# Decode attention: a slot's scores in four 32-column tiles, the maximum across quadrants by GpSimd, and no waits of TensorE on itself

## The chip, the cores and the metric

The kernel runs on one core of a Trainium2 chip. The metric is device time in microseconds; the time before is the median of three runs.

## The reference

Two layers of decode attention, each followed by a dense MLP, for a batch of 8 with one new token per row. Both layers use the same weights and the same K and V caches.

```python
def attention(x, k_cache, v_cache, wq, wo):      # x: 8 x 1 x 512
    q = (x @ wq).reshape(8, 1, 32, 128)          # 32 query heads of 128
    k = jnp.repeat(k_cache, 4, axis=1)           # 8 KV heads, 8192 keys each, 4 query heads per KV head
    v = jnp.repeat(v_cache, 4, axis=1)
    p = softmax(q . k * 128 ** -0.5)
    return (p . v) @ wo
x = x + attention(layernorm(x)); x = x + silu(layernorm(x) @ w1) @ w2     # w1: 512 x 1792
x = x + attention(layernorm(x)); x = x + silu(layernorm(x) @ w1) @ w2
```

All inputs are bfloat16. K and V hold 134 MB each. What must be computed for every one of 8 x 8 (batch row, KV head) pairs and both layers is a softmax over 8192 keys for 4 query heads.

## The kernel before

**Tasks, positions, slots.** A task is one (layer, batch row, KV head): 128 tasks in all, in an order that `make_tasks` writes out, with the two layers interleaved. A task's 8192 keys are four granules of 2048 keys (`NGRAN`), each granule fills a 512 KB slot of an arena in SBUF with 27 slots (`NSLOT`), and each slot has two halves of 1024 keys. The main loop (L722) goes over positions `p`, one half each, so a task has eight positions. Of the 32 granules of keys of a batch row, the last 18 (`KEEP`) stay in the arena from layer 0 to layer 1, already transposed; a layer-1 task on those heads loads V alone.

**Loads.** All loads of K and V are issued by SyncE (L326, called from `issue`), in an order that `plan_loads` fixes beforehand by the position at which each is needed. K is needed `LT` = 3 positions ahead of its scores, V is used `LP` = 14 positions after its scores. Each load waits until the former content of its slot has been used; `issue_until(p)` at the end of a position issues what may follow.

**What a position does,** in the order of emission:

- `emit_t_until(p + 3)`: eight 128x128 transposes of raw keys on TensorE into one of three PSUM banks (L420), then one copy of 128x1024 back over the slot's half, by VectorE (L428, five of eight) or ScalarE (L426, three of eight). Kept keys skip this.
- `emit_s(p)`: the scores of the half. Two matmuls (L455) with 512 keys as the moving operand each. The stationary operand is a window of 128 columns out of `QB`, in which a task's four query vectors stand 16 columns apart, with zeros between them; the window is shifted by the block's number j, so that block j's scores of query r land in PSUM row 16r + j, and the 16 matmuls of a task add up in one bank of 64 used rows by 512.
- `emit_pv(p - 14)`: eight matmuls (L517) of 128 stationary V columns against 32 moving columns of P.
- a softmax step of the task before, by phase: phase 0 the maximum (L464 to L474: a row maximum of 64x512 out of PSUM, then a 32x32 transpose, a small maximum, a scaling and a second transpose, all on VectorE, so that each row gets the maximum of its query); phase 1 the exp on ScalarE with the row sums (L478); phase 3 the sums (L484 on VectorE, then a sum across partitions on GpSimd, L487); phase 4 the transposes of P (L496) and their copy out of PSUM (L500); phase 7 the reciprocal (L504).
- where due, one step of a batch row's chain between the layers: output projection (L604), layer norm (L539 to L573, with two GpSimd reductions, L541 and L556), MLP and next queries (L586).

**Waits.** `Sync.acquire` (L90) collects, for every resource that an operation reads or writes, the marks of the last writer and of the readers since, keeps the highest mark per engine, and emits a wait for each, for the operation's own engine as well. Each engine takes its instructions in order.

Of the kernel before, what the change touches and what calls it, by code (L numbers as in the profile page):

```python
# [7 lines left out]
SM_SCALE = DH ** -0.5  # L8
# [19 lines left out]
PVN = 8  # L28
CW = 32
SETTLE = 2  # L30
ACT_EVAC = (1, 4, 7)

BF16 = mybir.dt.bfloat16
# [25 lines left out]
class Sync:  # L59
# [30 lines left out]
    def acquire(self, eng, reads=(), writes=()):  # L90
        toks = []
        for r in reads:
            if r.last_write is not None:
                toks.append(r.last_write)
        for r in writes:
            if r.last_write is not None:
                toks.append(r.last_write)
            toks.extend(r.reads)
        best = {}
        for t in toks:  # L100
            k = t.sem
            if k not in best or best[k].val < t.val:
                best[k] = t
        for t in best.values():
            self.wait(eng, t)

    def release(self, tok, reads=(), writes=()):
        for r in reads:
# [96 lines left out]
def _build(ctx, nc, A_x, A_k_cache, A_v_cache, A_wq, A_wo, B_w1, B_w2, out):  # L205
# [7 lines left out]
    NCH = S // 128  # L213
    NGRAN = NCH // (GRP * GPG)
    SLOT = GRP * GPG * 128
    assert GPT * GRP == NCH and NGRAN * GPG == GPT and KT * 128 == D and FT * 128 == F

    order = [(g, k) for g in range(HKV) for k in range(NGRAN)]
    kept = set(order[len(order) - KEEP:])
# [14 lines left out]
    def sb(shape, dt, name):  # L234
        _cnt[0] += 1
        return ctx.enter_context(nc.sbuf_tensor(f"{name}_{_cnt[0]}", shape, dt))
# [19 lines left out]
    w2_sb = sb([128, FT, D], BF16, "w2")  # L256
    ident = sb([128, 128], BF16, "ident")
    XT = [sb([128, KT, B], BF16, f"XT{n}") for n in range(3)]
    NJ = NCH * 128 // KB
    NR = NJ * REP  # L260
    CPB = KB // 128
    JPG = GRP * 128 // KB
    assert NR <= 128 and NJ % 16 == 0 and JPG * KB == GRP * 128
    QT1 = sb([128, B * HQ], BF16, "QT1")
    QT2 = [sb([128, HQ], BF16, "QT2") for _ in range(2)]
    QB = [sb([128, NJ - 1 + 128], BF16, "QB") for _ in range(NQB)]
    at1 = [sb([128, HQ], BF16, "at1") for _ in range(3)]
    at2 = sb([128, HQ, B], BF16, "at2")
    vr = sb([128, B], FP32, "vr")
# [9 lines left out]
    assert KB == D  # L279
    P = sb([128, KB], BF16, "P")  # L280
    Xr = P
    PT = [sb([128, CPB, NR], BF16, "PT") for _ in range(NPT)]
    hm = sb([NR, REP], FP32, "hm")
    mxa = sb([NR, 32], FP32, "mxa")
    mxb = sb([NR, 32], FP32, "mxb")
    mxh = sb([NR, 32 // NJ], FP32, "mxh")
    rs = [sb([NR, 1], FP32, "rs") for _ in range(NST)]
    ssm = [sb([128, REP], FP32, "ssm") for _ in range(NST)]
    ssa = [sb([128, REP], FP32, "ssa") for _ in range(NST)]
    rcp = [sb([128, REP], FP32, "rcp") for _ in range(NST)]  # L290
# [18 lines left out]
    def r_half(slot, h):  # L309
        return res(f"slot{slot}_{h}")  # L310

    def op(eng, inst_fn, reads=(), writes=()):
        reads = [res(n) if isinstance(n, str) else n for n in reads]
        writes = [res(n) if isinstance(n, str) else n for n in writes]
        syn.acquire(eng, reads, writes)
        inst = inst_fn()
        tok = syn.mark(inst, eng)
        syn.release(tok, reads, writes)
        return tok
# [31 lines left out]
    with nc.Block() as block:  # L351

        @block.sync
        def _(sync_eng):
# [8 lines left out]
                ),  # L363
                reads=["ident"], writes=["ident"],
            )
            op(dve, lambda: dve.memset(P[NR:128, :], 0.0), writes=["Pz"])
            op(dve, lambda: dve.memset(mxa[:, :], 0.0), writes=["mxa"])
            for n in range(NQB):
                op(pool, lambda n=n: pool.memset(QB[n][:, :], 0.0), writes=[f"QB{n}"])
            for n in range(NST):  # L370
                op(pool, lambda n=n: pool.memset(ssm[n][:, :], 0.0), writes=[f"ssm{n}"])
            op(
                dve,
                lambda: dve.tensor_reduce(
                    hm[:, :], ident[0:NR, 0:NR].rearrange("p (r j) -> p r j", j=NJ), AX.X, ALU.add),
                reads=["ident"], writes=["hm"],
            )

            queue = list(loads)

# [55 lines left out]
            def emit_q(ti):  # L436
                layer, b, g = tasks[ti]
                if layer == 0:
                    q, rq = QT1[:, b * HQ + g * REP:b * HQ + (g + 1) * REP], "QT1"
                else:  # L440
                    q, rq = QT2[b % 2][:, g * REP:(g + 1) * REP], f"QT2_{b % 2}"
                qb = QB[ti % NQB][:, 0:REP * NJ].rearrange("p (r j) -> p r j", j=NJ)[:, :, NJ - 1]
                op(act, lambda: act.copy(qb, q), reads=[rq], writes=[f"QB{ti % NQB}"])  # L443

            def emit_s(i):
                ti = i // GPT
                b, g, k, h = where(i)
                slot = k_slot[(b, g, k)]
                bank, qn = ti % NSCP, ti % NQB
                keys = half(slot, h)  # L450
                steps = []
                for c in range(JPG):
                    j = (i % GPT) * JPG + c
                    steps.append(
                        lambda c=c, j=j: pe.matmul(  # L455
                            SCp[bank][:, :], QB[qn][:, NJ - 1 - j:NJ - 1 - j + 128], keys[:, c * KB:(c + 1) * KB],
                            start=(j == 0), stop=(j == NJ - 1),
                        )
                    )
                mm_group(steps, reads=[r_half(slot, h), f"QB{qn}"], writes=[f"SC{bank}"])  # L460

            def softmax_max(ti):
                bank = ti % NSCP
                op(dve, lambda: dve.tensor_reduce(mxa[:, 0:1], SCp[bank][0:NR, :], AX.X, ALU.max),  # L464
                   reads=[f"SC{bank}"], writes=["mxa"])
                op(dve, lambda: dve.transpose(mxb[:, :], mxa[:, :]), reads=["mxa"], writes=["mxb"])  # L466
                op(dve, lambda: dve.tensor_reduce(
                    mxh[:, :], mxb[:, :].rearrange("p (r j) -> p r j", j=NJ), AX.X, ALU.max),
                   reads=["mxb"], writes=["mxh"])
                op(dve, lambda: dve.tensor_scalar(  # L470
                    mxa[:, :].rearrange("p (r j) -> p r j", j=NJ),
                    mxh[:, :].unsqueeze(2).to_broadcast([NR, 32 // NJ, NJ]), -SM_SCALE, None, op0=ALU.mult),
                   reads=["mxh"], writes=["mxa"])
                op(dve, lambda: dve.transpose(mxb[:, :], mxa[:, :]), reads=["mxa"], writes=["mxb"])  # L474

            def softmax_exp(ti):
                bank, st = ti % NSCP, ti % NST
                op(act, lambda: act.activation(  # L478
                    P[0:NR, :], SCp[bank][0:NR, :], ACT.Exp, bias=mxb[:, 0:1], scale=SM_SCALE, accum_out=rs[st][:, :]),
                   reads=[f"SC{bank}", "mxb"], writes=["P", f"rs{st}"])  # L480

            def softmax_sum(ti):
                st = ti % NST
                op(dve, lambda: dve.tensor_scalar(  # L484
                    ssm[st][0:NR, :], hm[:, :], rs[st][:, 0:1], None, op0=ALU.mult),
                   reads=["hm", f"rs{st}"], writes=[f"ssm{st}"])
                op(pool, lambda: pool.partition_all_reduce(ssa[st][:, :], ssm[st][:, :], 128, bass.bass_isa.ReduceOp.add),  # L487
                   reads=[f"ssm{st}"], writes=[f"ssa{st}"])

            def emit_pt(ti):  # L490
                pb = ti % NPT
                tb = evacs[0] % NTP
                evacs[0] += 1
                tpv = TPp[tb][:, 0:KB].rearrange("p (c q) -> p c q", q=128)
                steps = [
                    lambda c=c: pe.transpose(tpv[:, c, :], P[:, c * 128:(c + 1) * 128], ident[:, :])  # L496
                    for c in range(CPB)
                ]
                mm_group(steps, reads=["P", "Pz", "ident"], writes=[f"TP{tb}"])
                op(dve, lambda: dve.tensor_copy(PT[pb][:, :, :], tpv[:, :, 0:NR]), reads=[f"TP{tb}"], writes=[f"PT{pb}"])  # L500

            def softmax_rcp(ti):
                st = ti % NST
# [2 lines left out]
            def emit_pv(i):  # L506
                ti = i // GPT
                b, g, k, h = where(i)
                slot = v_slot[(b, g, k)]
                ob, pb = ti % 2, ti % NPT  # L510
                pv = PT[pb][:, :, :].rearrange("p c (r j) -> p c j r", j=NJ)
                otp = OTp[ob][:, 0:REP * PVN].rearrange("p (r n) -> p r n", n=PVN)
                steps = []
                for c in range(GRP):
                    cc = (i % GPT) * GRP + c
                    steps.append(
                        lambda c=c, cc=cc: pe.matmul(  # L517
                            otp, chunk(slot, h * GRP + c), pv[:, cc % CPB, cc // CPB, :].unsqueeze(2).to_broadcast([128, REP, PVN]),
                            start=(cc == 0), stop=(cc == NCH - 1),
                        )  # L520
                    )
                mm_group(steps, reads=[r_half(slot, h), f"PT{pb}"], writes=[f"OT{ob}"])

# [283 lines left out]
```

## Time and profile before

| what | us |
|---|---|
| three runs | 1232.51, 1233.66, 1235.64 |
| median | 1233.66 |
| profiled execution: span from first to last instruction | 1235.5 |
| TensorE matmul busy, of the span | 1123.1 (91%) |
| VectorE busy | 627.3 (51%) |
| ScalarE busy | 391.5 (32%) |
| GpSimd busy | 70.9 (6%) |
| mean granted clock of TensorE | 0.982 of full |

The span of the profiled execution lies by the slowest of the three runs. 476 MB go through the DMA engines, nearly all of it K and V. PE is TensorE's matmuls, PEld its weight loads, DVE VectorE, ACT ScalarE, POOL GpSimd, SP SyncE and SPq its queue. An engine row of the timeline reads: start, length, engine, line, operation, output and inputs, shapes, count, and in brackets how long the engine had been idle and what ended that. A matmul's length in the trace includes its way through the array, so the pace of a stream of matmuls is read from the distance of their starts. A row of the windows view gives, for a stretch, the busy time of PE, PEld, DVE, ACT and POOL with counts, then the granted clock, the share of the DMA engines and GB/s.

### The profile page before, as it was taken

What the parts mean: (1) busy time and instruction counts of PE and PEld (TensorE: products, weight loads), DVE (VectorE), ACT (ScalarE), POOL (GpSimd) and SP (SyncE); (2) the same over time, 40 slices, a digit from 0 to 9 for tenths busy, and PEclk for the clock granted to TensorE, in tenths of its full rate; (3) what the DMA queues carried; (4) which work ended last, traced back from release to release, by engine and by line L of the source; (5) the groups of instructions that cost most, each with busy time, mean ns of one, the idle gap of its engine ahead of it and who ended that gap; (6) DMA issues with size and microseconds to landing.
All of it is one profiled execution on the core that took longest, in us unless ns stands there. A gap on an engine that the chain in (4) does not pass through costs nothing.

```text
span 1235.5 us, 45818 instructions
## 1 busy us (share of the span) xinstructions
PE 1123.1 (91%) x19620; PEld 870.5 (70%) x19960; DVE 627.3 (51%) x1977; ACT 391.5 (32%) x670; POOL 70.9 (6%) x176
## 2 busy tenths in 40 slices
PE   2899999999999899989998899999999899999996
PEld 2577777777677677767677777777677777778764
DVE  2445554556355554546455554555455554556543
ACT  1233332333233332333233332333233322333320
POOL 0000000000000000000000000000000000000000
PEclk8899999999999999999999999999999999999997
DMA  9999999999999999999999999999999999999993
GB/s 374 385 398 405 397 370 408 408 402 383 381 408 407 386 353 409 408 382 375 388 408 401 370 366 409 408 403 374 377 408 396 369 351 408 409 403 394 391 407 151
DMA packets 133928, 476.45 MB, mean 386 GB/s; under 512 B 14160, under 2 KB 20064, under 8 KB 133216
## 3 DMA queue, kind: packets, MB, share of 16 engines
q1 hardware_dynamic: 133728, 473.51, 98.3%
q8 instruction: 159, 2.61, 0.8%
q14 instruction: 41, 0.34, 0.1%
HBM read 473.44 MB, written 0.01 MB: 383 GB/s over the span
## 4 chain that ended last, share of the span: by engine, by line
PE 47%; DMA 40%; SPq 6%; DVE 3%; issue 3%; POOL 0%; ACT 0%; POOLq 0%; DVEq 0%
DMA arena<-in_A_k_cache_dram 38%; PE SCp L455 20%; PE TPp L420 12%; PE OTp L517 9%; SPq L326 6%; PE MISC L586 4%; DMA wo<-in_A_wo_dram 2%; PE MISC L604 1%; PE TPp L496 1%; DVE arena L428 1%; DVE mxa L464 0%; DVE mxb L466 0%; DVE tr L568 0%; DVE yr L571 0%; DVE tr L569 0%
## 5 line engine op out<-in xcount | busy, mean ns | idle before, releaser
L455 PE MATMUL SCp<-arena,QB 128*128 128x512 bf16 x1708 | 540.4, 382 | 22.4 <-ACT QB L443 2.0
L517 PEld LDWEIGHTS OTp<-PT,arena 128*128 128x128 bf16 x8192 | 354.1, 96 | 243.4 <-issue 8.0
L420 PE MATMUL TPp<-ident,arena 128*128 128x128 bf16 x5888 | 453.1, 220 | 62.0 <-DMA arena<-in_A_k_cache_dram 39.8
L428 DVE COPY arena<-TPp 128x1024 bf16<-128x1024 bf16 x460 | 316.9, 690 | 352.3 <-PE TPp L420 352.1
L426 ACT COPY arena<-TPp 128x1024 bf16<-128x1024 bf16 x276 | 279.3, 1012 | 610.6 <-PE TPp L420 610.5
L420 PEld LDWEIGHTS TPp<-ident,arena 128*128 128x128 bf16 x5888 | 339.3, 98 | 87.1 <-DMA arena<-in_A_k_cache_dram 60.2
L517 PE MATMUL OTp<-PT,arena 128*128 128x32 bf16 x8192 | 363.5, 177 | 1.8 <-DMA arena<-in_A_v_cache_dram 0.5
L455 PEld LDWEIGHTS SCp<-arena,QB 128*128 128x128 bf16 x2048 | 148.1, 98 | 6.2 <-PE SCp L455 3.8
L478 ACT ACTIVATE P<-SCp,mxb 64x512 bf16<-64x512 f32 x128 | 87.3, 682 | 186.8 <-DVE mxb L474 164.4
L487 POOL PARTITION_ALL_REDUCE ssa<-ssm x128 | 55.6, 434 | 1045.7 <-DVE ssm L484 978.2
L464 DVE TENSOR_REDUCE mxa<-SCp 64x1 f32<-64x512 f32 x128 | 85.5, 668 | 29.6 <-PE SCp L455 29.6
L500 DVE COPY PT<-TPp 128x256 bf16<-128x256 bf16 x128 | 37.2, 291 | 94.6 <-PE TPp L496 94.6
L496 PE MATMUL TPp<-ident,P 128*128 128x128 bf16 x512 | 49.0, 217 | 0.0
L484 DVE TENSOR_SCALAR ssm<-hm,rs 64x4 f32<-64x4 f32 x128 | 27.6, 216 | 36.5 <-ACT P L478 36.5
L604 PE MATMUL MISC<-at,wo 128*128 128x32 bf16 (+1 forms) x1152 | 39.8, 175 | 4.1 <-DMA wo<-in_A_wo_dram 3.5
L604 PEld LDWEIGHTS MISC<-at,wo 128*128 128x128 bf16 x1152 | 33.9, 96 | 4.9 <-DMA wo<-in_A_wo_dram 3.6
L586 PE MATMUL MISC<-xnT,wq 128*128 128x32 bf16 (+1 forms) x1152 | 34.7, 175 | 2.5 <-issue 2.4
L586 PEld LDWEIGHTS MISC<-xnT,wq 128*128 128x128 bf16 x1152 | 31.7, 96 | 2.9 <-issue 2.8
L443 ACT COPY QB<-QT 128x4 bf16<-128x4 bf16 x128 | 26.3, 206 | 11.6 <-DVE QT L669 11.6
L496 PEld LDWEIGHTS TPp<-ident,P 128*128 128x128 bf16 x512 | 29.6, 96 | 0.2
L531 DVE TENSOR_TENSOR at<-OTp,rcp 128x4 bf16<-128x4 f32 x128 | 21.0, 164 | 15.4 <-PE OTp L517 15.4
L474 DVE STREAM_TRANSPOSE mxb<-mxa 64x32 f32<-64x32 f32 x128 | 26.1, 204 | 4.4
(46 smaller groups left out, 258.4 us busy)
## 6 DMA issues: line engine op xcount, KB each, us to landing
arena<-in_A_v_cache_dram SPq DMA_DIRECT2D x512, 512.0 KB, 10.1
arena<-in_A_k_cache_dram SPq DMA_DIRECT2D x368, 512.0 KB, 14.4
wq<-in_A_wq_dram SPq DMA_DIRECT2D x1, 4096.0 KB, 16.3
wo<-in_A_wo_dram SPq DMA_DIRECT2D x1, 4096.0 KB, 25.9
w<-in_B_w_dram SPq DMA_DIRECT2D x2, 1792.0 KB, 22.5
P<-in_A_x_dram SPq DMA_DIRECT2D x1, 8.0 KB
out_dram<-P SPq DMA_DIRECT2D x1, 8.0 KB
```

What stands on the lines that cost most here:

```text
L326: eng.dma_start(out_ap, in_ap).then_inc(counter.sem, 16)
L420: lambda c=c: pe.transpose(tpv[:, c, :], chunk(slot, h * GRP + c), ident[:, :])
L426: op(act, lambda: act.copy(dst, TPp[tb][:, :]), reads=[f"TP{tb}"], writes=[r_half(slot, h)])
L428: op(dve, lambda: dve.tensor_copy(dst, TPp[tb][:, :]), reads=[f"TP{tb}"], writes=[r_half(slot, h)])
L455: lambda c=c, j=j: pe.matmul(SCp[bank][:, :], QB[qn][:, NJ - 1 - j:NJ - 1 - j + 128], keys[:, c * KB:(c + 1) * KB], start=(j == 0), stop=( ...
L464: op(dve, lambda: dve.tensor_reduce(mxa[:, 0:1], SCp[bank][0:NR, :], AX.X, ALU.max), reads=[f"SC{bank}"], writes=["mxa"])
L478: op(act, lambda: act.activation(P[0:NR, :], SCp[bank][0:NR, :], ACT.Exp, bias=mxb[:, 0:1], scale=SM_SCALE, accum_out=rs[st][:, :]), reads ...
L487: op(pool, lambda: pool.partition_all_reduce(ssa[st][:, :], ssm[st][:, :], 128, bass.bass_isa.ReduceOp.add), reads=[f"ssm{st}"], writes=[f ...
L496: lambda c=c: pe.transpose(tpv[:, c, :], P[:, c * 128:(c + 1) * 128], ident[:, :])
L517: lambda c=c, cc=cc: pe.matmul(otp, chunk(slot, h * GRP + c), pv[:, cc % CPB, cc // CPB, :].unsqueeze(2).to_broadcast([128, REP, PVN]), st ...
L586: lambda o=o, k=k: pe.matmul(MISC[:, o * n:o * n + w], w_sb[:, k, o * 128:(o + 1) * 128], rhs_of(k).to_broadcast([128, w]) if n == 1 else ...
L604: lambda o=o, h=h: pe.matmul(MISC[:, o * w:(o + 1) * w], wo_sb[:, h, o * 128:(o + 1) * 128], rhs_of(h).to_broadcast([128, w]) if n == 1 el ...
```

## The change

**Scores.** A granule's scores are now computed at once, at its second half's position: four matmuls of 512 keys, each with 32 stationary columns instead of 128, and each in a column tile of its own (`tile_position=(0, 32 t)`), writing PSUM rows 32t to 32t + 31. `QB`'s queries stand 4 columns apart and the window is shifted by the granule k, so query r, granule k, block t land in row 32t + 4r + k. 16 rows of each quadrant of 32 are used; the other rows hold zero scores.

**Maximum.** After the row maximum (now of 128x512) VectorE adds a mask (`hneg`, 0 where a row belongs to the query of that column, -1e30 elsewhere) to make a 128x4 tile, GpSimd takes the maximum across all partitions, and at phase 1 VectorE picks each row's value with a multiplication by `hsc` and a sum over four columns. The two 32x32 transposes, the small maximum and the scaling between them go. The buffers of this are four deep (`NST`).

**The rest of softmax.** exp, row sums and mask work on 128 rows; the copy of P's transposes takes 16 of each 32 columns, and `emit_pv` indexes it accordingly.

**Waits.** `acquire` no longer emits a wait of TensorE on TensorE's own marks.

```diff
--- before.py
+++ after.py
@@ -28,6 +28,7 @@
 SETTLE = 2
+MASKED = 1e30
 ACT_EVAC = (1, 4, 7)
@@ -101,8 +102,10 @@
                 best[k] = t
+        own = self.eng_sem[eng.engine] if eng is self.nc.tensor else None
         for t in best.values():
-            self.wait(eng, t)
+            if t.sem is not own:
+                self.wait(eng, t)
@@ -213,7 +216,7 @@
     SLOT = GRP * GPG * 128
-    assert GPT * GRP == NCH and NGRAN * GPG == GPT and KT * 128 == D and FT * 128 == F
+    assert GPT * GRP == NCH and GPG == 2 and NGRAN * GPG == GPT and KT * 128 == D and FT * 128 == F
@@ -256,14 +259,13 @@
     XT = [sb([128, KT, B], BF16, f"XT{n}") for n in range(3)]
-    NJ = NCH * 128 // KB
-    NR = NJ * REP
+    NT = 4
+    QR = 32
     CPB = KB // 128
-    JPG = GRP * 128 // KB
-    assert NR <= 128 and NJ % 16 == 0 and JPG * KB == GRP * 128
+    assert NT * KB == SLOT and NGRAN * REP <= QR and NT * QR == 128
     QT1 = sb([128, B * HQ], BF16, "QT1")
     QT2 = [sb([128, HQ], BF16, "QT2") for _ in range(2)]
-    QB = [sb([128, NJ - 1 + 128], BF16, "QB") for _ in range(NQB)]
+    QB = [sb([128, NGRAN - 1 + QR], BF16, "QB") for _ in range(NQB)]
     at1 = [sb([128, HQ], BF16, "at1") for _ in range(3)]
@@ -279,12 +281,16 @@
     Xr = P
-    PT = [sb([128, CPB, NR], BF16, "PT") for _ in range(NPT)]
-    hm = sb([NR, REP], FP32, "hm")
-    mxa = sb([NR, 32], FP32, "mxa")
-    mxb = sb([NR, 32], FP32, "mxb")
-    mxh = sb([NR, 32 // NJ], FP32, "mxh")
-    rs = [sb([NR, 1], FP32, "rs") for _ in range(NST)]
+    PT = [sb([128, CPB, NT, NGRAN * REP], BF16, "PT") for _ in range(NPT)]
+    hm = sb([128, REP], FP32, "hm")
+    hneg = sb([128, REP], FP32, "hneg")
+    hsc = sb([128, REP], FP32, "hsc")
+    mxp = [sb([128, 1], FP32, "mxp") for _ in range(NST)]
+    mxr = [sb([128, REP], FP32, "mxr") for _ in range(NST)]
+    mxa = [sb([128, REP], FP32, "mxa") for _ in range(NST)]
+    nbr = sb([128, REP], FP32, "nbr")
+    nb = [sb([128, 1], FP32, "nb") for _ in range(NST)]
+    rs = [sb([128, 1], FP32, "rs") for _ in range(NST)]
     ssm = [sb([128, REP], FP32, "ssm") for _ in range(NST)]
@@ -363,18 +369,18 @@
-            op(dve, lambda: dve.memset(P[NR:128, :], 0.0), writes=["Pz"])
-            op(dve, lambda: dve.memset(mxa[:, :], 0.0), writes=["mxa"])
             for n in range(NQB):
...
-            for n in range(NST):
-                op(pool, lambda n=n: pool.memset(ssm[n][:, :], 0.0), writes=[f"ssm{n}"])
             op(
...
-                    hm[:, :], ident[0:NR, 0:NR].rearrange("p (r j) -> p r j", j=NJ), AX.X, ALU.add),
+                    hm[:, :], ident[:, :].rearrange("p (t r k) -> p r t k", t=NT, k=NGRAN)[:, 0:REP], AX.XY, ALU.add),
                 reads=["ident"], writes=["hm"],
...
+            op(dve, lambda: dve.tensor_scalar(hneg[:, :], hm[:, :], -1.0, MASKED, op0=ALU.add, op1=ALU.mult),
+               reads=["hm"], writes=["hneg"])
+            op(dve, lambda: dve.tensor_scalar(hsc[:, :], hm[:, :], -SM_SCALE, None, op0=ALU.mult),
+               reads=["hm"], writes=["hsc"])
@@ -439,50 +445,49 @@
                     q, rq = QT2[b % 2][:, g * REP:(g + 1) * REP], f"QT2_{b % 2}"
-                qb = QB[ti % NQB][:, 0:REP * NJ].rearrange("p (r j) -> p r j", j=NJ)[:, :, NJ - 1]
+                qb = QB[ti % NQB][:, NGRAN - 1:NGRAN - 1 + REP * NGRAN:NGRAN]
...
                 b, g, k, h = where(i)
+                if h != GPG - 1:
+                    return
                 slot = k_slot[(b, g, k)]
                 bank, qn = ti % NSCP, ti % NQB
-                keys = half(slot, h)
-                steps = []
-                for c in range(JPG):
-                    j = (i % GPT) * JPG + c
-                    steps.append(
-                        lambda c=c, j=j: pe.matmul(
-                            SCp[bank][:, :], QB[qn][:, NJ - 1 - j:NJ - 1 - j + 128], keys[:, c * KB:(c + 1) * KB],
-                            start=(j == 0), stop=(j == NJ - 1),
-                        )
+                keys = ARENA[:, slot * SLOT:(slot + 1) * SLOT]
+                steps = [
+                    lambda t=t: pe.matmul(
+                        SCp[bank][t * QR:(t + 1) * QR, :], QB[qn][:, NGRAN - 1 - k:NGRAN - 1 - k + QR],
+                        keys[:, t * KB:(t + 1) * KB], start=(k == 0), stop=(k == NGRAN - 1),
+                        tile_position=(0, t * QR),
...
-                mm_group(steps, reads=[r_half(slot, h), f"QB{qn}"], writes=[f"SC{bank}"])
+                    for t in range(NT)
+                ]
+                mm_group(steps, reads=[r_half(slot, 0), r_half(slot, 1), f"QB{qn}"], writes=[f"SC{bank}"])
             def softmax_max(ti):
-                bank = ti % NSCP
-                op(dve, lambda: dve.tensor_reduce(mxa[:, 0:1], SCp[bank][0:NR, :], AX.X, ALU.max),
-                   reads=[f"SC{bank}"], writes=["mxa"])
-                op(dve, lambda: dve.transpose(mxb[:, :], mxa[:, :]), reads=["mxa"], writes=["mxb"])
-                op(dve, lambda: dve.tensor_reduce(
-                    mxh[:, :], mxb[:, :].rearrange("p (r j) -> p r j", j=NJ), AX.X, ALU.max),
-                   reads=["mxb"], writes=["mxh"])
-                op(dve, lambda: dve.tensor_scalar(
-                    mxa[:, :].rearrange("p (r j) -> p r j", j=NJ),
-                    mxh[:, :].unsqueeze(2).to_broadcast([NR, 32 // NJ, NJ]), -SM_SCALE, None, op0=ALU.mult),
-                   reads=["mxh"], writes=["mxa"])
-                op(dve, lambda: dve.transpose(mxb[:, :], mxa[:, :]), reads=["mxa"], writes=["mxb"])
+                bank, st = ti % NSCP, ti % NST
+                op(dve, lambda: dve.tensor_reduce(mxp[st][:, :], SCp[bank][:, :], AX.X, ALU.max),
+                   reads=[f"SC{bank}"], writes=[f"mxp{st}"])
+                op(dve, lambda: dve.tensor_scalar(mxr[st][:, :], hneg[:, :], mxp[st][:, 0:1], None, op0=ALU.add),
+                   reads=["hneg", f"mxp{st}"], writes=[f"mxr{st}"])
+                op(pool, lambda: pool.partition_all_reduce(mxa[st][:, :], mxr[st][:, :], 128, bass.bass_isa.ReduceOp.max),
+                   reads=[f"mxr{st}"], writes=[f"mxa{st}"])
...
                 bank, st = ti % NSCP, ti % NST
+                op(dve, lambda: dve.tensor_tensor(nbr[:, :], mxa[st][:, :], hsc[:, :], ALU.mult),
+                   reads=[f"mxa{st}", "hsc"], writes=["nbr"])
+                op(dve, lambda: dve.tensor_reduce(nb[st][:, :], nbr[:, :], AX.X, ALU.add),
+                   reads=["nbr"], writes=[f"nb{st}"])
...
-                    P[0:NR, :], SCp[bank][0:NR, :], ACT.Exp, bias=mxb[:, 0:1], scale=SM_SCALE, accum_out=rs[st][:, :]),
-                   reads=[f"SC{bank}", "mxb"], writes=["P", f"rs{st}"])
+                    P[:, :], SCp[bank][:, :], ACT.Exp, bias=nb[st][:, 0:1], scale=SM_SCALE, accum_out=rs[st][:, :]),
+                   reads=[f"SC{bank}", f"nb{st}"], writes=["P", f"rs{st}"])
...
                 st = ti % NST
-                op(dve, lambda: dve.tensor_scalar(
-                    ssm[st][0:NR, :], hm[:, :], rs[st][:, 0:1], None, op0=ALU.mult),
+                op(dve, lambda: dve.tensor_scalar(ssm[st][:, :], hm[:, :], rs[st][:, 0:1], None, op0=ALU.mult),
                    reads=["hm", f"rs{st}"], writes=[f"ssm{st}"])
@@ -496,8 +501,9 @@
                 ]
-                mm_group(steps, reads=["P", "Pz", "ident"], writes=[f"TP{tb}"])
-                op(dve, lambda: dve.tensor_copy(PT[pb][:, :, :], tpv[:, :, 0:NR]), reads=[f"TP{tb}"], writes=[f"PT{pb}"])
+                mm_group(steps, reads=["P", "ident"], writes=[f"TP{tb}"])
+                op(dve, lambda: dve.tensor_copy(
+                    PT[pb][:, :, :, :], tpv.rearrange("p c (t q) -> p c t q", q=QR)[:, :, :, 0:NGRAN * REP]), reads=[f"TP{tb}"], writes=[f"PT{pb}"])
@@ -508,14 +514,13 @@
                 ob, pb = ti % 2, ti % NPT
-                pv = PT[pb][:, :, :].rearrange("p c (r j) -> p c j r", j=NJ)
                 otp = OTp[ob][:, 0:REP * PVN].rearrange("p (r n) -> p r n", n=PVN)
...
-                            otp, chunk(slot, h * GRP + c), pv[:, cc % CPB, cc // CPB, :].unsqueeze(2).to_broadcast([128, REP, PVN]),
+                            otp, chunk(slot, h * GRP + c), PT[pb][:, cc % CPB, (cc // CPB) % NT, cc // (CPB * NT)::NGRAN].unsqueeze(2).to_broadcast([128, REP, PVN]),
                             start=(cc == 0), stop=(cc == NCH - 1),
...

```

## The prediction

> **What bounds the kernel now.** I read four views: the page's rates by slice, the waits of SyncE's queue, the timeline of a stretch with K and V loads and of one with V loads alone, and the busy times by window around the places where the clock drops.
>
> The page first: GB/s in 40 slices of 30.9 us, and the load queue's share of the 16 DMA engines.
>
> ```profile
> GB/s 374 385 398 405 397 370 408 408 402 383 381 408 407 386 353 409 408 382 375 388 408 401 370 366 409 408 403 374 377 408 396 369 351 408 409 403 394 391 407 151
> q1 hardware_dynamic: 133728, 473.51, 98.3%
> ```
>
> The reader is to see a ceiling, 408 to 409, which a third of the slices touch, and dips to 351. The queue is nearly always busy, so transfers are the floor; the dips are where something keeps them from the ceiling. Summed over slices 3 to 39, (408 - rate) makes 576; times 30.9 us, over 408, that is **43.6 us** of lost transfer time. What SyncE waits for says who holds the loads back (total us, times, longest):
>
> ```profile
> SPq L87 <- PE SCp L455: 280.5, 152, 4.6
> SPq L87 <- PE OTp L517: 173.4, 100, 3.7
> ```
>
> A load waits for the scores or the values product to give a slot back. Whether TensorE is the limit there, or itself waits for data, depends on the stage. A slot of 512 KB (0.524 MB) at 408 GB/s is 1.285 us of transfer. A task with K and V loads takes eight, 10.28 us; one whose keys are kept (V alone) takes four, 5.14 us. TensorE's pace, first with K and V, then with V alone:
>
> ```profile
> 241.73 0.59 PE L455 MATMUL SCp<-arena,QB 128*128 128x512 bf16 x2
> 242.16 0.35 PE L517 MATMUL OTp<-PT,arena 128*128 128x32 bf16 x8
> 242.37 0.61 PE L420 MATMUL TPp<-ident,arena 128*128 128x128 bf16 x8
> 242.81 0.59 PE L455 MATMUL SCp<-arena,QB 128*128 128x512 bf16 x2
> ...
> 594.71 0.59 PE L455 MATMUL SCp<-arena,QB 128*128 128x512 bf16 x2
> 595.14 0.35 PE L517 MATMUL OTp<-PT,arena 128*128 128x32 bf16 x8
> 595.45 0.59 PE L455 MATMUL SCp<-arena,QB 128*128 128x512 bf16 x2
> 595.88 0.35 PE L517 MATMUL OTp<-PT,arena 128*128 128x32 bf16 x8
> ```
>
> Starts, not durations, give the pace: scores 0.43 us (two of 0.216), values 0.20 (eight of 0.025), transposes 0.44: 1.08 per position with K, about 0.66 to 0.75 without. At the end of the run, tasks with V alone follow each other every 5.89 us (normalisations L531 at 1195.23, 1201.12, 1207.01). Scores are 4 slots x 0.86 = 3.44 of that, so a V-alone task needs **2.45 + 4x** us of TensorE, with x the cost of a slot's scores; a K-and-V task, 8 x 1.08 plus some 0.6 for the transposes of P and the output projection, needs **5.8 + 4x** = 9.2. So K-and-V stages are bound by transfers (9.2 against 10.28), V-alone stages by TensorE (5.89 against 5.14). 18 of 32 granules are kept: 64 x 18/32 = 36 V-alone tasks lose 0.75 each, 27 us; the other 17 of the 43.6 fall in the stretches where a batch's MLP chain adds matmuls (1.78 between positions at 290.32 and 292.10 instead of 1.08).
>
> **The change, part by part.** *Scores in column tiles.* Count and moving length stay (2048 matmuls of 512 columns), but the four of a slot go to four 32-column strips and may run side by side. No row shows that. Lower bound of x: 0.216 + 3 x 0.025 (the closest starts in the trace) = 0.29. Upper bound: one after another, 0.86, plus two switches between full width and strips, in which the array empties: a 128x32 matmul lasts 177 ns where starts are 25 apart, so 0.15 is left in the pipe, and a weight load of 98 ns is then uncovered: 2 x 0.25. That makes 1.36. Strips that run together with both switches paid give 0.79. I take **x = 0.45**, four together plus one emptying of 0.15, nearest to the 0.216 row because nothing in a strip changes the rate at which its columns stream.
>
> On the hiding of weight loads, these two rows stand side by side:
>
> ```profile
> 241.29 0.61 PE L420 MATMUL TPp<-ident,arena 128*128 128x128 bf16 x8
> ...
> 241.68 0.15 PEld L455 LDWEIGHTS SCp<-arena,QB 128*128 128x128 bf16 x2
> ```
>
> The scores' weights load while transposes still run, both on all 128 rows. [...]
>
> With x = 0.45, K-and-V needs 7.6 of 10.28, V-alone 4.25 of 5.14: both below the transfers. The score group now waits for both halves of a slot and is issued at the odd position; it frees the slot at the position where it did before, so the plan of loads and SyncE's order are unchanged.
>
> *Maximum by GpSimd.* Out go four VectorE operations per task (204, 178, 174, 204 ns, 0.24 apart more or less), in come one on 128x4 before GpSimd's reduction and two behind it (near the 216 ns of L484 and the 168 of L504). VectorE's work falls by some 0.2 us, at 51% busy worth nothing. GpSimd's reduction for a maximum is in no row; the sum is:
>
> ```profile
> 423.86 0.40 POOL L556 PARTITION_ALL_REDUCE s1a<-s  x1 [0.69 <-DVE s L554]
> ...
> 424.29 0.15 DVE L561 TENSOR_SCALAR vr<-s1a 128x1 f32<-128x1 f32 x1
> ```
>
> 0.43 us from its start to its reader's. I take 0.55 with both hops; at the ends, 0.4 and, if a maximum takes another path, several us (a rival). The new wait stands at VectorE's first operation of the exp step: queued behind it are the next transposes' evacuation and the exp on ScalarE, and TensorE waits for those. One evacuation (0.69) usually stands ahead of the wait and covers it; where ScalarE has the evacuation, or there is none, VectorE stands 0.3 to 0.5 us. The path from the last score to P was 2.36 us (593.03 to the end of ScalarE's read, 595.39); now 0.67 + 0.2 + 0.55 + 0.2 + 0.2 + 0.15 + 0.87 = 2.85. TensorE has five value groups and two score slots before it needs P: 1.0 + 0.9 = 1.9. In a V-alone task it then stands 1.0, which before was hidden, and the task takes 4.25 + 1.0 = 5.25: just over the 5.14 of transfer. This is what is late next.
>
> *No waits on itself.* Waits of TensorE on its own work sum to some 6 us in the waits view (3.8 scores, 1.0 values, 1.0 projection). In the last 7 us, where value groups stand alone, each group takes 0.49 of which 0.16 to 0.23 is such a gap. Gain 2 to 3 us there, in parallel with the tail below; elsewhere nothing.
>
> *Set-up, P's copy.* A few memsets go and two small VectorE operations come beside the first loads, nothing. P's copy reads runs of 16 instead of 64 columns, 0.29 to perhaps 0.42 us; covered except in V-alone tasks, inside the allowance below.
>
> **The sum**, against the profiled span of 1235.5 us (runs 1232.51 to 1235.64, median 1233.66, so the result is set 1.8 lower). V-alone: 36 x (5.89 - 5.25) = 23. MLP stretches: per position a K-and-V task leaves 1.285 - 7.6/8 = 0.33 us for them instead of 0.13; over the some 20 positions of a chain that is 6.6, against 240 matmuls x 0.025 = 6; I take 11 of 17. Tail: transfers are at full rate until about 1213 and the last values end at 1221.2, then 14 us of serial work that stays; a TensorE that keeps up ends two groups behind the last landing; I take 6 of 8. Together 40: 1195.5, less 1.8 gives **1194**.
>
> **Rivals.** (A, forecast) x from 0.29 to 0.65: 1183 to 1208. All 43.6 and 8 recovered would be 1183.9 - 1.8 = 1182.
>
> (B) Strips run together but every switch empties the array, x = 0.79. For it: 0.15 us really is in the pipe behind each group. V-alone 5.61: 36 x 0.28 = 10, the stretches 5, tail 2: 1217. [...]
>
> (C) Nothing gained, x near 0.86: the strips do not overlap and the switches are free, so the split does not do what it says. 1230 to 1237.
>
> (D) Slower: strips one after another and both switches paid, x = 1.36, in every one of 512 slots. V-alone 7.89, +2.0 x 36 = 72; K-and-V 11.24, over its transfers by 0.96 x 92 = 88: about 1394. It decides from x = 0.9 in V-alone stages (14 us per 0.1) and from 1.12 in the others; at 1.1 it gives 1268. Against it: strips use different columns and different outputs.
>
> (E) GpSimd's maximum costs 3 us instead of 0.43: V-alone tasks stand 2.6 longer, 36 x 2.5 = 90 less what is gained, and some K-and-V tasks too: about 1290.
>
> (F) The clock. It halves after a slack stretch, as here (PE busy, and the granted clock after the POOL column):
>
> ```profile
> 699.60:703.00 3.40, 1.38 (x25) 0.97 (x21) 2.98 (x16) 1.12 (x2) 0.25 (x1) 1.00 1.02 404
> 703.00:706.50 3.50, 3.38 (x54) 2.87 (x55) 1.16 (x4) 0.00 (x0) 0.45 (x1) 0.51 0.91 337
> ```
>
> 1.38 us busy of 3.4 was followed by 3.4 at half speed. TensorE with more slack will do this often. At half speed it becomes busy and returns, so each costs at most about 1 us of transfers; ten of them move A by 10 us, to 1204. It lies within A.
>
> **Chances.** A 0.54, B 0.18, C 0.06, D 0.17, E 0.05. Within 0.3% is about what a measurement can tell from no change: faster 0.72, same 0.06, slower 0.22. The likeliest case's own range is 1182 to 1208. For 8 in 10, the range must take in B and C and D's mild end (x up to 1.07): 1180 to 1262; outside are 0.15 of D and E and 0.04 below.
>
> **What would show it.** Right: the rates' dips of 350 to 385 rise above 400; starts of the four score matmuls of a slot lie near 25 ns apart, and the next group starts within 0.5 us of the first; SyncE's waits on L455's successor shrink while TensorE's waits on K landings grow; V-alone tasks come every 5.1 to 5.3 us. Wrong: starts 0.2 us apart in a slot (C or D); gaps of 0.2 us around each score group (B); a maximum reduction on GpSimd of over 1 us (E); the clock row at 5 over whole slices (F).

## The result, and the profile after

The changed kernel takes **1219.92 us** (median of four runs, 1216.6 to 1222.07) against 1234.2 for the kernel before on the same chip: ratio 0.9874, 95% interval 0.9852 to 0.9896. It is faster, by 14 us where 40 were forecast: inside the range given (1180 to 1262), far from its value of 1194. The profiled execution has a span of 1216.8 us, 18.7 less than before; that is 4 more than the medians differ, since the profiled execution of before was its slowest.

Rates by slice, the load queue's share, and the granted clock in tenths, from the page of the changed kernel:

```profile
GB/s 369 385 397 407 406 384 408 408 404 394 381 408 408 399 347 409 408 404 403 377 408 408 397 365 409 409 402 397 394 408 407 388 375 407 409 402 399 392 408 172
q1 hardware_dynamic: 133728, 473.51, 99.1%
...
PEclk8789998999799998999899999999899998999996
```

The dips are still where they were, most of them shallower (the sixth slice went from 370 to 384, the 33rd from 351 to 375), but not the two at 353 and 366, now 347 and 365. From 25 to 470 MB landed, the transfers took 1134.4 us before and 1117.4 after; at 0.408 MB per us they would take 1090.7. So **43.7 us were lost before and 26.7 are lost now**. The 17.0 recovered and 1.9 behind the 470 MB, less 0.3 ahead of the first 25, are the 18.7 of the spans.

The pace of TensorE, first with K and V, then among the last V-alone tasks:

```profile
234.04 0.62 PE L426 MATMUL TPp<-ident,arena 128*128 128x128 bf16 x8 [0.42 <-DMA arena<-in_A_k_cache_dram]
234.59 0.10 PEld L460 LDWEIGHTS SCp<-arena,QB 128*32 128x32 bf16 x4
234.59 0.40 PE L460 MATMUL SCp<-arena,QB 128*32 128x512 bf16 x4
234.92 0.27 PEld L522 LDWEIGHTS OTp<-PT,arena 128*128 128x128 bf16 x8 [0.23 <-issue]
...
1181.53 0.17 DVE L536 TENSOR_TENSOR at<-OTp,rcp 128x4 bf16<-128x4 f32 x1 [0.34 <-PE OTp L522]
...
1186.65 0.17 DVE L536 TENSOR_TENSOR at<-OTp,rcp 128x4 bf16<-128x4 f32 x1 [0.34 <-PE OTp L522]
```

Four score matmuls all start and end within 0.40 us, their starts 3 to 4 ns apart and each 0.39 us long (0.38 before): the strips run together. The next group's weights start 0.33 behind, after a gap of 0.23 that is new. V-alone tasks at the end follow each other every 5.12 us, the time of their four transfers. TensorE waits for keys far more than before (39.8 us then), and a new kind of wait has appeared ("issue"):

```profile
PE TPp L426 <- DMA arena<-in_A_k_cache_dram: 145.6, 248, 1.4
PEld OTp L522 <- issue: 129.6, 509, 1.4
```

The second stands behind the strips, at the first full-width weights: 509 times for 512 slots. SyncE's waits for the scores to give a slot back, which were to shrink, went from 280.5 us only to 257.6.

### The profile page after: what moved, and what is told of

The parts are those of the page before. It is cut to its first block, busy times and chain, and to the rows that moved or that the text cites. A ratio compares the mean times of both kernels' runs of the same rounds, so it can differ in the third digit from the quotient of the medians.

```text
span 1216.8 us, 45763 instructions
## 1 busy us (share of the span) xinstructions
PE 969.7 (80%) x19960; PEld 747.1 (61%) x19960; DVE 594.5 (49%) x1849; ACT 388.8 (32%) x670; POOL 117.7 (10%) x300
## 4 chain that ended last, share of the span: by engine, by line
DMA 61%; PE 24%; SPq 7%; DVE 4%; issue 3%; POOL 0%; ACT 0%; POOLq 0%; ACTq 0%; DVEq 0%
DMA arena<-in_A_k_cache_dram 51%; PE TPp L426 9%; DMA arena<-in_A_v_cache_dram 8%; SPq L332 7%; PE OTp L522 5%; PE SCp L460 4%; PE MISC L591 4%; DMA wo<-in_A_wo_dram 2%; DVE arena L434 1%; PE MISC L609 1%; PE TPp L501 1%; DVE tr L573 0%; DVE yr L576 0%; DVE tr L574 0%; DVE mxp L471 0%
## 5 line engine op out<-in xcount | busy, mean ns | idle before, releaser
L426 PE MATMUL TPp<-ident,arena 128*128 128x128 bf16 x5888 | 463.0, 223 | 170.9 <-DMA arena<-in_A_k_cache_dram 145.6
L522 PEld LDWEIGHTS OTp<-PT,arena 128*128 128x128 bf16 x8192 | 285.9, 97 | 166.8 <-issue 129.6
L460 PE MATMUL SCp<-arena,QB 128*32 128x512 bf16 x2048 | 217.7, 415 | 3.5 <-ACT QB L449 1.6
L484 ACT ACTIVATE P<-SCp,nb 128x512 bf16<-128x512 f32 x128 | 88.0, 687 | 223.3 <-DVE nb L482 203.6
L475 POOL PARTITION_ALL_REDUCE mxa<-mxr x128 | 47.5, 371 | 666.5 <-DVE mxr L473 628.3
L471 DVE TENSOR_REDUCE mxp<-SCp 128x1 f32<-128x512 f32 x128 | 86.6, 677 | 15.1 <-PE SCp L460 15.1
L460 PEld LDWEIGHTS SCp<-arena,QB 128*32 128x32 bf16 x2048 | 53.5, 94 | 51.4 <-issue 7.3
L490 DVE TENSOR_SCALAR ssm<-hm,rs 128x4 f32<-128x4 f32 x128 | 28.6, 223 | 36.7 <-ACT P L484 36.7
L480 DVE TENSOR_TENSOR nbr<-mxa,hsc 128x4 f32<-128x4 f32 x128 | 20.4, 160 | 41.0 <-POOL mxa L475 41.0
L473 DVE TENSOR_SCALAR mxr<-hneg,mxp 128x4 f32<-128x4 f32 x128 | 29.4, 230 | 4.6
```

The source lines that it names most:

```text
L426: lambda c=c: pe.transpose(tpv[:, c, :], chunk(slot, h * GRP + c), ident[:, :])
L460: lambda t=t: pe.matmul(SCp[bank][t * QR:(t + 1) * QR, :], QB[qn][:, NGRAN - 1 - k:NGRAN - 1 - k + QR], keys[:, t * KB:(t + 1) * KB], star ...
L471: op(dve, lambda: dve.tensor_reduce(mxp[st][:, :], SCp[bank][:, :], AX.X, ALU.max), reads=[f"SC{bank}"], writes=[f"mxp{st}"])
L484: op(act, lambda: act.activation(P[:, :], SCp[bank][:, :], ACT.Exp, bias=nb[st][:, 0:1], scale=SM_SCALE, accum_out=rs[st][:, :]), reads=[f ...
L522: lambda c=c, cc=cc: pe.matmul(otp, chunk(slot, h * GRP + c), PT[pb][:, cc % CPB, (cc // CPB) % NT, cc // (CPB * NT)::NGRAN].unsqueeze(2). ...
```

## The experiments

The table adds up what the traces hold: transfer time lost between 25 and 470 MB landed (against 408 GB/s); time at half clock between 60 and 1190 us; and TensorE's gaps of over 0.45 us (in 60 to 1180 us) at an instruction that waits for no semaphore.

| kernel | ratio to before (95%) | lost us | half clock us | unwaited gaps |
|---|---|---|---|---|
| before | 1 | 43.7 | 10 | 5, 3.9 us |
| after | 0.9874 (0.9852 to 0.9896) | 26.7 | 101 | 12, 13.4 us |
| e1 before, no chain | 0.9748 (0.9723 to 0.9773) | 9.7 | 8 | 0 |
| e2 after, no chain | 0.9729 (0.9699 to 0.9759) | 9.3 | 123 | 0 |
| e3 after, waits put back | 0.9966 (0.9949 to 0.9982) | 36.4 | 188 | 20, 22.5 us |
| e4 after, norm split | 0.9900 (0.9873 to 0.9928) | 31.0 | 120 | 11, 10.7 us |
| e5 before, no self-waits | 0.9943 (0.9922 to 0.9963) | 36.1 | 7 | 1, 0.8 us |
| e6 after, chain ready | 0.9884 (0.9858 to 0.9910) | 29.0 | 133 | 13, 14.6 us |
| e7 after, chain cut | 0.9744 (0.9719 to 0.9768) | 10.3 | 144 | 1, 0.6 us |
| e8 after, no maximum | 0.9844 (0.9812 to 0.9877) | 27.6 | 137 | 15, 17.0 us |
| e9 after, chain cut and wide | 0.9761 (0.9729 to 0.9792) | 12.9 | 116 | 0 |
| e10 after, fine parts | 0.9909 (0.9887 to 0.9931) | 34.1 | 157 | 6, 4.3 us |
| e11 e9 with waits put back | 0.9798 (0.9772 to 0.9824) | 18.2 | 188 | 3, 3.3 us |
| e12 before, chain cut and wide | 0.9926 (0.9907 to 0.9945) | 32.7 | 10 | 0 |
| e13 before, chain cut | 0.9762 (0.9744 to 0.9779) | 13.5 | 10 | 0 |

**Where the loss was: e1 and e2.** The chain of a batch row is reduced to two copies (`only`: XT2 from XT0, and QT2 from QT1).

```diff
-                st = block_stages(xs, ["XT0", "XT1", "XT2"], 1, True)
...
+                return [only]
```

> The kernel before, with each batch row's chain between the layers left out (layer norms, MLP, next queries; a copy of the first queries stands for them). It leaves out that part of the computation. As predicted on record, V-alone tasks lose 27 us of transfer time at TensorE's pace and the MLP stretches 17: then 1234 - 17 = 1217 us. New theory: V-alone tasks lost nothing, since the arena lets the loads run ahead in them, and nearly all of the 44 us lost belongs to the stretches with the chain: then 1195 to 1205 us.

> The changed kernel with the same chain left out. New theory: the 27 us of transfer time that it still loses are the chain's too, so about 1190 to 1197 us, only some 5 us below the kernel before without its chain (the tail). As predicted on record (V-alone tasks gain 23): some 20 us below the kernel before without its chain.

1203.14 us and 1200.72; e2 lies above the 1190 to 1197 expected of it, since 9.3 us are lost without the chain too. Without it, the kernel before loses as little as the changed one, with TensorE as slow in V-alone tasks as ever, as a row of e1 among them shows:

```profile
583.00:598.00 15.00, 14.62 (x229) 9.88 (x232) 5.59 (x25) 2.63 (x9) 1.29 (x3) 1.00 1.03 408
```

The recorded theory (1217) falls. Of the 43.7 us lost, 34 go with the chain, and so does all but 2.4 us of the change's gain.

**The waits on itself: e3 and e5.**

```diff
-            if t.sem is not own:
-                self.wait(eng, t)
+            self.wait(eng, t)
```

> The changed kernel with TensorE's waits on itself put back. If they cost only where value groups stand alone, 0 to 3 us slower than the change (1220 to 1223). A rival: with short score groups the waits meet work still in the array at each slot, 0.2 us x 512, partly on the path: 1230 or more, and then they are what most of the gain comes from.

> The kernel before with only one part of the change: no waits of TensorE on itself. In the trace of before these waits leave some 6 us of gaps, nearly all near the start and the end, and its clock is at half for only 10 us: if the waits cost through the work they cover, 0 to 4 us faster (1230 to 1234). Rival: they cost before what they cost in the changed kernel, 10 us: 1224.

1230.53 us for e3, the rival's figure: with the waits back, the strips and GpSimd's maximum gain only 0.3%. 1227.22 for e5, between the two expectations: alone, the waits' removal gains 0.6%. The parts together give more (1.3%) than their sum (0.9%), by about what the intervals leave open. In both pairs the kernel with the waits has more unwaited gaps and loses more, and e3 spends 188 us at half clock.

**VectorE's block and the chain's waits: e4 and e6.**

```diff
-                return [first, second, third]
+                return [first, second, third] + [newton] * (NEWTON - 1) + [last]
```

> The changed kernel with the last stage of a layer norm (13 VectorE operations in a row, 2.6 us, in which P's copy and the evacuations queue) cut into three stages of four or five operations, one per position. If that block, and the half clock that follows the stall of TensorE behind it, is what loses transfers in the chain's stretches: 5 to 10 us faster (1210 to 1215). If the chain's own matmuls are the limit there: within 2 us of 1220.

```diff
+                if n == 1:
+                    rhs_of, r_rhs = lambda k: QT1[:, k:k + 1], "QT1"
```

> The changed kernel with the per-row chain's matmuls (MLP and next queries) reading the first queries instead of the normalised rows, so that TensorE never waits for the chain's VectorE work; the chain's results are not the reference's. All its operations stay. If those waits lose the transfers: 1205 to 1212. If the matmuls' own time does: 1217 to 1221.

1221.55 us and 1219.87: nothing. The edit of e4 makes four stages of three or four operations, not three of four or five. In e4, TensorE's wait behind the block shrinks from 9.7 to 1.3 us, and a wait of the MLP for the norm (9.2) takes its place.

**The chain's matmuls, their time or their instructions: e7, e9, e12, e13.**

```diff
+                if n == 1:
+                    kparts = 1
-                w = CW if n == 1 else n
+                w = 256 if n == 1 else n
```

The change of `w` is in e9, e11 and e12 only. The cut leaves 50 of the chain's 240 matmuls, so 190 go, not the 110 to 180 of e7's expectation.

> The changed kernel with the chain's contractions cut to their first block of 128 (the first of 4 or 14), 110 fewer to 180 fewer matmuls per batch row; the rest of each sum is left out. Waits on the chain's VectorE work stay. If the matmuls' time loses the transfers in the chain's stretches: 1203 to 1210. If the waits do: 1215 to 1221.

> The changed kernel with the chain's contractions cut to their first block of 128 as before (the rest of each sum is left out), but each matmul streaming 256 columns (107 ns at full clock) instead of 32 (25 ns): a chain then has 50 matmuls x 0.107 = 5.3 us of TensorE time, about the 6 us of the 240 in the changed kernel, with a fifth of their instructions. If the chain costs through TensorE's time: 1216 to 1221. If it costs through the fetching of its instructions (gaps inside a group that waits for nothing, each with a 16 KB packet on the instruction queue that ends some 1.4 us before TensorE goes on): 1202 to 1208, and those gaps are gone.

> The kernel before with the chain's contractions cut to their first block (the rest of each sum left out) and each matmul 256 columns wide, so that the chain keeps its TensorE time and has a fifth of its instructions. In the kernel before a task with K and V needs 9.2 us of TensorE, 11.3 with its share of a chain, against 10.28 of transfer. If that time is the limit: little is gained, 1225 to 1234. If fetches are the limit here too: 1205 to 1213.

> The kernel before with the same contractions cut, matmuls 32 columns wide: a fifth of the chain's instructions and of its TensorE time. If time is the limit in the chain's stretches: 1205 to 1213, some 20 us below the wide one. If the limit is the chain's waits on VectorE: 1225 or more.

On the changed kernel 1202.15 (cut; just under what was expected) and 1206.91 us (cut, but as long): the time hardly matters, the number of instructions does. Each matmul that goes takes its weight load along, and no run separates the two. On the kernel before 1206.65 and 1226.80: there the time is the larger limit, as the sums said (11.3 us of TensorE per task against 10.28). The waits of TensorE by cause in e9, between 100 and 1180 us, all but the smallest:

```profile
PE TPp L426 <- DMA arena<-in_A_k_cache_dram: 146.5, 248, 1.7
PE OTp L522 <- DMA arena<-in_A_v_cache_dram: 18.3, 62, 0.8
PE TPp L426 <- DVE ssm L490: 9.6, 6, 2.1
PE TPp L501 <- ACT P L484: 3.4, 5, 1.0
```

and the rows of the changed kernel in the same stretch that have no counterpart there:

```profile
PE MISC L591 <- issue: 5.7, 6, 1.7
PE TPp L426 <- issue: 4.0, 3, 1.8
PE OTp L522 <- issue: 3.3, 4, 1.3
PE SCp L460 <- issue: 1.2, 1, 1.2
```

**The rest: e8, e10, e11.** e8 drops the maximum's five operations and sets the bias to zero. e10: `SETTLE = 4`, groups of 14 and 16 matmuls. e11 is e9 with the wait line of e3.

> The changed kernel without the maximum (exp with a zero bias; the row maximum, the mask, GpSimd's maximum and the two operations behind it are left out). Theory: VectorE has slack and P comes early enough, so 0 to 4 us faster (1216 to 1220). Rival, VectorE's wait for GpSimd holds evacuations and P back in the chain's stretches: 8 us or more faster.

> The changed kernel, complete, with the chain's matmul groups cut into half as large ones (14 or 16 instead of 28 or 32), so that they spread over more positions, and four idle steps instead of two behind a layer norm. If bursts are what costs (of time or of fetches): 3 to 8 us faster than the change, 1212 to 1217. If it is the total: within 2 us of 1220.

> The wide, short chain of the run before with TensorE's waits on itself put back. In the full changed kernel these waits cost 10 us and went with more gaps at instruction fetches. If they cost through the fetches: within 3 us of the run before. If through the array standing still at each slot, or the clock: 8 to 12 us slower than it.

e8: 1215.82 us; its interval overlaps that of the change, so the maximum costs 0 to 8 us and most likely 4. e10: 1225.49, outside both expectations and no gain. The unwaited gaps do fall, to 4.3 us, but two chain steps now share a position, and TensorE waits 12.3 us for the norm and 9.1 for an evacuation ahead of P's transposes. e11: 1211.89, slower than e9 by 0.4% of before where the waits cost 0.9% in the full kernel; neither expectation holds alone, roughly half of their cost goes with the chain's instructions. No version that computes everything beat the changed kernel.

## Why the prediction was wrong, and where it was right

**The score's cost was right.** A slot takes two positions; from one score group to the next they take 1.73 us where nothing holds TensorE up, against 2 x 1.08 before: x is 0.86 - 0.43 = 0.43, where 0.45 was taken. Both switches cost time: behind the strips the next weights start after a gap of 0.23 us, and strips begin 0.11 us later than a full-width group would (0.55 from the transposes' start instead of 0.44). Over the 0.216 of one stream that is 0.11 on either side, a little under half of the 0.25 per switch in rival B. That the array empties at a switch, from which the 0.15 was estimated (177 ns of a matmul less the 25 between starts), no run shows; the trace of the changed kernel shows these two delays. The forecast's terms were others (0.29 for starts 25 ns apart and 0.15 for one switch), so that they came to nearly the same was in part luck. B's own sum leaves out the 1.0 us of standing that the forecast's 5.25 has.

**The failing step is "V-alone: 36 x (5.89 - 5.25) = 23".** The pace was read rightly for the end of the run (in mid-run it is mostly 5.49), and its price wrongly. TensorE was busy throughout those tasks, but the transfers lost nothing in them, since each consumed granule of kept keys frees a slot of the arena and the loads run ahead into it. The windows view of before, which was there to be read ahead of the change, shows it, in V-alone stretches in the middle and at the end of the run (the last two numbers are DMA share and GB/s):

```profile
598.00:613.00 15.00, 14.65 (x226) 9.73 (x228) 6.11 (x25) 2.63 (x9) 1.17 (x3) 1.00 1.03 412
1183.00:1201.00 18.00, 17.45 (x301) 12.49 (x308) 7.02 (x27) 3.53 (x10) 1.29 (x3) 1.00 1.03 408
```

TensorE is busy nearly throughout and the rate is at its ceiling. Nor did these tasks become shorter: the 28 of them among tasks 9 to 122 took 5.98 us each before and 6.01 after, in which the rate brings 4.7 slots where a task needs four, of V. Lost transfer time by kind of task (from one row maximum to the next, tasks 9 to 122; each sum is good to about 1 us):

| task | before | after |
|---|---|---|
| 28 V-alone | -0.8 | -0.4 |
| 23 K and V with MLP matmuls | 28.9 | 17.4 |
| 21 other K and V of that stretch | 9.6 | 5.5 |
| 7 partly kept | 4.7 | 3.4 |
| 35 layer 0 with kept keys | 0.3 | 0.1 |

So the V-alone term was 0 instead of 23; the stretches held nearly all of the 44 instead of 17, and gave back 17 where 11 were taken; the tail gave 1.9 instead of 6. The 1.0 us by which TensorE was to stand for P in every V-alone task is not there either: between 100 and 1180 us it waits for P 8 times, 6.6 us in all.

**What is late next, in those stretches.** By the sums, TensorE at 7.6 + 83 x 0.025 = 9.7 us per task had become faster than the 10.28 of transfer, and the whole loss should have gone. A task with MLP matmuls takes 11.38 in fact (11.90 before): TensorE stands for 1.5 of it, and 0.74 pass at half clock. One of the stands, in the timeline of the changed kernel:

```profile
441.88 0.25 PE L591 MATMUL MISC<-xnT,wq 128*128 128x32 bf16 x4
443.88 0.94 PE L591 MATMUL MISC<-xnT,wq 128*128 128x32 bf16 x28 [1.75 <-issue]
```

and the windows around it:

```profile
442.00:444.00 2.00, 0.25 (x11) 0.15 (x8) 0.57 (x1) 0.00 (x0) 0.00 (x0) 0.99 1.04 406
444.00:447.00 3.00, 3.00 (x71) 2.37 (x70) 0.83 (x2) 0.00 (x0) 0.37 (x1) 0.50 0.81 328
```

The gap lies inside one group of 32 matmuls, which waits for nothing. A 16 KB packet of the instruction queue ran from 441.4 to 442.4, and TensorE went on 1.4 us after it. While TensorE stands, loads already issued go on (406 GB/s); then SyncE waits for scores to give a slot back, and for three microseconds the rate is 328, at half clock. All 12 unwaited gaps of the changed kernel have such a packet that ends 1.2 to 1.6 us ahead of their end, and so have the 5 of before and the 20 of e3. e9 and e7 show that here the chain's instructions are the limit, e12 and e13 that before it was mostly TensorE's time. That the gaps themselves are the whole of it is not shown: they are 13.4 us of the 26.7 lost, and e10 cut them to 4.3, put other stands in their place, and lost more.

**Self-waits** were priced at 2 to 3 us in the tail; alone they were worth 6 (e5), and with the strips 11 (e3), and not in the tail: in e5 the transfer time lost between 25 and 470 MB falls from 43.7 to 36.1. They were read from the waits view, which in before shows 1.7 us of them between 100 and 1180 us (0.2 of matmuls, 1.5 of weight loads); in what the rest of their cost lies, no run shows. **GpSimd's maximum** was right: 0.40 us from its start to its reader, and VectorE stands 0.50 for it with both hops, where 0.55 was taken (rival E is out). P's copy took 0.29 us as before. A maximum in the changed kernel:

```profile
1183.35 0.37 POOL L475 PARTITION_ALL_REDUCE mxa<-mxr  x1 [2.70 <-DVE mxr L473]
1183.75 0.16 DVE L480 TENSOR_TENSOR nbr<-mxa,hsc 128x4 f32<-128x4 f32 x1 [0.50 <-POOL mxa L475]
```

**The clock** (rival F) came, 101 us at half speed against 10. Most of it lies in V-alone tasks (2.5 us of 6.0 each), where it costs no transfers. But there it came with much less slack than described; in two rows of the changed kernel,

```profile
594.20:597.60 3.40, 2.50 (x60) 1.72 (x56) 1.62 (x7) 0.49 (x1) 0.51 (x2) 1.00 1.01 406
597.60:601.00 3.40, 3.38 (x53) 1.71 (x49) 0.77 (x4) 0.38 (x3) 0.43 (x1) 0.50 1.03 420
```

TensorE was busy for 2.50 of the 3.40 us ahead of the half clock, against 1.38 in the prediction's row. What the clock goes by is not shown here; in both traces, of before and after, its records are 1.0 or 0.5, in pieces of 3.41 us and its multiples (the last piece apart, which runs past the end).

## What to carry to other kernels

A stage in which an engine is slower than the transfers cost nothing here while the transfers still ran at their ceiling: read the rate of that very stage (408 to 412 GB/s in the V-alone rows) before pricing the engine's excess. Where a buffer lets loads run ahead, look for the loss in a later stage that uses the lead up; here that took the chain's work as well (43.7 us lost with it, 9.7 without). After an engine's busy time is cut, look for what makes it stand for short times.

## What was not expected of the hardware

TensorE stood still at instructions that waited for nothing; that their instructions came late is an estimate from the 16 KB packet of the instruction queue that ends 1.2 to 1.6 us ahead of each gap's end, and no run isolated it. There were 12 gaps of 0.5 to 1.8 us, 13.4 in all, in stretches where 28 or 32 matmuls, 25 ns from start to start, stand in a row among the usual groups; before, at a slower pace, 5 gaps and 3.9 us. Cutting a chain from 240 matmuls to 50 at nearly the same TensorE time (50 x 0.11 us by their starts in e9, for 240 x 0.025) was worth 1.1% of the run in the changed kernel (0.9874 to 0.9761) and 0.7% in the kernel before. And the waits of TensorE on its own earlier work, of which the waits view of before shows 1.7 us between 100 and 1180 us, cost 0.6% before and 0.9% with the strips.
